# Gate products in four column groups with a summing product, the choice of expert behind the attention scores, memory rows spread one pair of values later

## The chip, the cores and the metric

The kernel runs on one core of a Trainium2 chip. The core has five engines that run their own instruction streams and wait for each other by semaphores: TensorE (PE, matrix products; its weight loads are listed as PEld), VectorE (DVE), ScalarE (ACT), GpSimd (POOL) and SyncE (SP, here only a queue of transfers). The metric is the device time of one execution in microseconds (us); lower is better. A tile below is 128 tokens.

## The reference, cut to what matters

The reference is a chunked attention followed by a mixture of experts with one expert a token.

```python
# attention: q, k, v (4, 8, 768, 64); mem_k, mem_v (4, 8, 8, 64); chunks of 32, context 16 left, 8 right
k_full = np.concatenate([mem_k, k_ctx], axis=2)
a = softmax(scale * q_c @ k_full^T);  out_c = a @ v_full
# moe: x (3072, 512), 8 experts, F = 512
h_dense = np.maximum(x @ w1_dense, 0.0);  y_dense = h_dense @ w2_dense
logits = x @ w_gate                      # (3072, 8), float32
expert_idx = np.argmax(logits, axis=1)
gate_w = 1 / sum(exp(logits - max))
y = y_dense + gate_w * (relu(x @ w1[e]) @ w2[e])     # e = expert_idx of the token
```

## The kernel before, in words

The program has two stages. The first (to about 155 us) computes the attention of 24 tiles of 128 tokens (four batches of six), the gate and the first dense product, and scatters each token's row to a table in memory that is ordered by expert. The second fetches 128 rows at a time by expert, multiplies, adds the second dense product and scatters the results to the output. The change touches the first stage only.

The order of all instructions is written by hand; each engine runs its own in the order of the program. The loop `for i in range(NT)` over the tiles is a software pipeline: pass i does the scores of tile i, but the values and the normalization of tile i-2, the transposition of x of tile i-3 (LAG_X), the gate of tile i-4 (LAG_G) and the dense product of tile i-5 (LAG_D). In pass i, PE runs in this order:

1. in the passes 2 to 17, one or two sets of twelve transposes that prepare keys (`kb`) or queries (`qb`) of the next batch (L353); their results are copied by ACT, two copies into `kbd` for a set of keys (L366), one into `qT` for a set of queries (L358). The second set of a pass comes at its end;
2. the dense product of tile i-5: four products of 512 columns (L469); ACT applies relu (L471);
3. the gate of tile i-4: for four blocks of 128 features, x is the stationary operand (128 x 128, float32) and the 8 columns of `w_gate` move; the four products sum in a PSUM tile `pg` that holds a group of three tiles (L462);
4. when the gate was the last of its group, `choose` follows on DVE (L484 to L494: maximum, difference, priority, maximum, one-hot `oh`), and on ACT three exponentials that also give the weight of each token (L497);
5. the transposes `turn` of the exponentials of tile i-1 (L411), copied by ACT to `aT` (L413);
6. the scores of tile i (L384, L390; L390 works in four column groups of 32). DVE takes the maximum (L399) and subtracts it (L401), ACT takes the exponential (L406);
7. `turn_x`, the transposes of x of tile i-3 (L449), copied by ACT to `x32` (L451); POOL casts that to bf16 (L454);
8. the values of tile i-2: 32 products in tiles of 64 x 32 (L423), normalized by DVE (L433, L435);
9. in every third pass (6, 9, 12, 15, 18, 21) `ranks`: products with `oh` that count each token's place (L504 to L512); DVE turns it into row numbers (`place`, L520, L523).

A window `vw` holds the values of two tiles (a pair; eight chunks) together with eight memory rows for each chunk. Its rows 32 to 56 are the first 24 rows of the next chunk, so they are copied from the window itself (`shift_v`, L308) and, for the last chunk, from the next window (L311, two copies of 24 x 260 in each odd pass). The windows are filled by transfers on SP's queue (`load_v`, L278); SP has also `spread_mem` (L297), which writes the memory rows, repeated for eight chunks, to a table `mrep` in memory, and the windows from the third on fetch their memory rows from it (L292); the first two take them from the SBUF tile `mtpl` (L287). POOL's queue issues the loads of keys and queries (L239), of expert and dense weights (L94), and the scatters (L529); POOL also casts x into the token's row (`keep_x`, L442, L443).

PSUM tiles of the pool `ps` have four buffers, shared by L353, L411, L390, L449 and the ranks; `pg` and the dense and value results have one buffer each.

Of the kernel before, what the change touches and what calls it, by code (L numbers as in the profile page):

```python
# [10 lines left out]
F32 = mybir.dt.float32  # L11
BF16 = mybir.dt.bfloat16
I32 = mybir.dt.int32
AF = mybir.ActivationFunctionType
# [12 lines left out]
PC = 8  # L27
# [17 lines left out]
GRP = 3  # L45
# [14 lines left out]
def kernel(  # L60
# [151 lines left out]
    with ExitStack() as one:  # L212
# [46 lines left out]
        def load_v(n):  # L259
            if n >= B * NP:  # L260
                return
            b, p = divmod(n, NP)
            vw = vws[n]
            if p == 0:
                for par in range(2):
                    r = 64 * par
                    eng = nc.gpsimd if n else nc.vector
                    eng.memset(vw[r:r + 32, 0, :, :D], 0.0)
                    eng.memset(ves[b][r:r + 32, :, :D], 0.0)
            lo = 1 if p == 0 else 0  # L270
            for par in range(2):
                r = 64 * par
                if p == 0:
                    hs = v[b].rearrange("(a c) s d -> c s a d", c=2)[par]
                    nc.sync.dma_start(vw[r + LEFT:r + 32, 0, :, :D], hs[0:LEFT])
                    nc.sync.dma_start(ves[b][r:r + LEFT, :, :D], hs[S - LEFT:S])
                for hp in range(HP):
                    nc.sync.dma_start(  # L278
                        vw[r:r + 32, lo:, hp, :D],
                        bass.AP(tensor=v.tensor,  # L280
                                offset=v[b, 2 * hp + par, CHUNK * (PC * p + lo) - LEFT, 0].offset,
                                ap=[[D, 32], [CHUNK * D, PC - lo], [1, D]]))
# [12 lines left out]
        def spread_mem():  # L295
            for par in range(2):
                nc.sync.dma_start(  # L297
                    mrep[:, par], mtpl[:, par].rearrange("p h d -> p (h d)")
                    .unsqueeze(1).to_broadcast([B * NMEM, PC, HP * (D + 1)]))

        def shift_v(n, par, last, eng=nc.vector.tensor_copy):
            if not 0 <= n < B * NP:
                return
            b, p = divmod(n, NP)
            r = 64 * par
            vw = vws[n]
            if not last:
                eng(vw[r + 32:r + 56, :PC - 1], vw[r:r + 24, 1:])  # L308
            else:
                nxt = ves[b][r:r + 24] if p == NP - 1 else vws[n + 1][r:r + 24, 0]  # L310
                eng(vw[r + 32:r + 56, PC - 1], nxt)  # L311

        def shift(i):

# [61 lines left out]
        def attention(g, qT, kbd):  # L376
# [80 lines left out]
                st["x32"], st["xT"] = x32, xT  # L457

            def gate():
                grp, u = st["grp"], st["u"]  # L460
                for d in range(DT):
                    nc.tensor.matmul(grp["pg"][:, u, :], st["x32"][:, d, :], wgate[:, d, :],  # L462
                                     start=(d == 0), stop=(d == DT - 1))

            def dense():
                late = g == NT - 2
                ph = (ps if late else pf).tile([128, F], F32, tag="ps" if late else "ph", name="ph")
                for d in range(DT):
# [2 lines left out]
                nc.scalar.activation(st["row"][:, XW:2 * XW].bitcast(BF16), ph, AF.Relu)  # L471

            return {"dense": dense, "scores": scores, "exp": expo, "turn": turn, "values": values, "norm": norm,
                    "keep_x": keep_x, "turn_x": turn_x, "gate": gate}

        def choose(grp):
            n = grp["n"]
# [15 lines left out]
            oh = small.tile([128, GRP, E], BF16, tag="oh", name="oh")[:, :n]  # L493
            nc.vector.tensor_tensor(oh, pr, wide(pm), ALU.is_equal)  # L494
            ex = small.tile([128, GRP, E], F32, tag="ex", name="ex")[:, :n]
            for u, row in enumerate(grp["rows"]):
                nc.scalar.activation(ex[:, u], df[:, u], AF.Exp, bias=0.0, scale=1.0,  # L497
                                     accum_out=row[:, ROW - 2:ROW - 1])
            grp["oh"] = oh

        def rank(grp, late):
            oh, n = grp["oh"], grp["n"]
# [49 lines left out]
        nc.vector.memset(kbds[0], 0.0)  # L552
        nc.vector.memset(mkbd, 0.0)
        make_identity(nc, identf)
        nc.sync.dma_start(wgate, moe_w_gate.rearrange("(t p) m -> p t m", p=128))
        load_v(1)
        spread_mem()
        turned, steps = transposes(0)
        for n, step in enumerate(steps):
            step()  # L560
# [21 lines left out]
            if 0 <= g < NT:  # L582
                parts[g][part]()

        def gates(g, now=True):
            grp, u = group_of.get(g, (None, 0))
            if grp is None:
                return
            n = grp["n"]
# [3 lines left out]
            if now:  # L593
                pick(g)

        def pick(g):
            grp, u = group_of.get(g, (None, 0))
            if grp is not None and u == grp["n"] - 1:
                grp["rows"] = [tiles[g - u + k]["row"] for k in range(u + 1)]
                choose(grp)  # L600

        def count_rows(cp):
            for t in range(GRP):
# [14 lines left out]
        for i in range(NT):  # L618
# [9 lines left out]
            tiles[i]["grp"], tiles[i]["u"] = group_of[i]  # L628
            for _ in range(qk_at.get(i, 0)):
                load_qk()  # L630
            if i == 3:
                load_w(E, 0)
            if i == 2:
                nc.gpsimd.memset(front_rows(), 1.0)
            if i in W_AT:
                next_w()
            if i == 1:
                load_v(2)
            if i == 1 or i == 3:
                load_v((i + 5) // 2)  # L640
            if i > 3 and i % 2 == 0:
# [30 lines left out]

        n = NT - 1
        early_fetch()
        gates(n - 3, now=False)
        do("keep_x", n - 2)
        do("turn", n)
        pick(n - 3)
        do("values", n - 1)
        do("turn_x", n - 2)  # L680
        do("norm", n - 1)
# [17 lines left out]
        ranks(n - 1)  # L699
        pick(n)  # L700
        scatter(n - 2)
        do("dense", n - 1)
        ranks(n)
# [250 lines left out]
```

## Time and profile before

| | us |
|---|---|
| median of three runs | 260.94 |
| the three runs | 260.94, 265.48, 260.94 |
| the profiled execution | 261.37 |
| its span from first to last instruction | 259.4 |
| attention stage, tiles 4 to 23 | 35 to 153 |

The granted clock of PE was 0.969 on average. The share of the span in which the engines were busy: PE 83%, DVE 64%, ACT 58%, POOL 57%.

Rows of the time line have the start in us from the beginning of the span, the duration from the first to the last instruction of the row, the engine, the line, the operation, what it writes and reads, its shape and the number of instructions; brackets give the idle time of the engine before the row and what ended it. "issue" there means that the engine waited for nothing that the profile shows. Rows of groups by line have the total busy time, the mean duration of one in ns, and the idle time before them. Instructions of PE overlap, so the cost of a block of products is read from the difference of two starts, not from its duration.

### The profile page before, as it was taken

The page shows a single profiled execution, that of the slowest core. Times are in us where ns is not written, and L with a number is a line of the kernel's source. Part 1 is how long each engine was busy: PE and PEld are TensorE (multiplying, and loading weights), DVE is VectorE, ACT ScalarE, POOL GpSimd, SP SyncE. Part 2 cuts the span into 40 slices and gives each one's busy share as a digit, 9 for nine tenths or more (in the row PEclk, how much of TensorE's full clock was granted, in tenths as well). Part 3 has the DMA queues.
Part 4 walks back from the last instruction along what each step waited for, and adds up shares of the span by engine and source line. Part 5 has one row for each costly group of instructions (what it writes and reads, how often), then busy time and mean ns, then how long its engine had stood idle before and what let it go on. Part 6 is the DMA issues. An engine that isn't in the chain of part 4 may idle for free. (4 is left out here: it accounts for less than half of the span.)

```text
span 259.4 us, 9762 instructions
## 1 busy us (share of the span) xinstructions
PE 215.6 (83%) x3843; PEld 160.2 (62%) x3843; DVE 166.3 (64%) x421; ACT 149.3 (58%) x279; POOL 148.1 (57%) x228
## 2 busy tenths in 40 slices
PE   1556869999798998969888797999999997999930
PEld 0335657778676876848666665766657764666610
DVE  7557855898788798997688534874554443555520
ACT  2545766767788677755667363555546654555520
POOL 8928651888576977865767554554545442334420
PEclk9999997999999999976999999999999999999995
DMA  6999996599989896999998484699999999351120
GB/s 82 189 204 171 161 197 112 111 190 179 183 164 198 136 238 148 135 252 248 280 187 162 141 174 180 173 222 297 276 267 217 286 294 290 124 162 56 48 112 3
DMA packets 56257, 47.03 MB, mean 181 GB/s; under 512 B 30190, under 2 KB 48366, under 8 KB 56048
## 3 DMA queue, kind: packets, MB, share of 16 engines
q0 software_dynamic: 22656, 28.38, 56.2%
q1 hardware_dynamic: 33552, 17.99, 29.4%
q8 instruction: 32, 0.52, 0.9%
q14 instruction: 17, 0.14, 0.2%
HBM read 46.60 MB, written 16.29 MB: 242 GB/s over the span
## 5 line engine op out<-in xcount | busy, mean ns | idle before, releaser
L868 POOL DMA_INDIRECT out_dram<-o,to x28 | 31.1, 1111 | 50.9 <-DVE o L866 41.3
L866 DVE TENSOR_TENSOR o<-py,oe 128x512 f32<-128x512 f32 x28 | 19.4, 691 | 30.2 <-ACT oe L864 28.6
L802 ACT COPY xT<-xt 128x512 bf16<-128x512 bf16 x28 | 16.4, 586 | 36.9 <-DVE gw L857 20.5
L529 POOL DMA_INDIRECT xs<-row,si x24 | 27.8, 1160 | 9.9 <-issue 6.3
L842 PE MATMUL py<-wall,h 128*128 128x512 bf16 (+1 forms) x112 | 28.7, 379 | 1.9 <-DMA wall<-in_moe_w_dram 1.9
L454 POOL CAST xT<-x 128x512 bf16<-128x512 f32 x22 | 13.6, 618 | 28.1 <-ACT x L451 27.9
L839 PE MATMUL py<-wall,xT 128*128 128x512 bf16 x112 | 28.8, 379 | 0.0
L462 PEld LDWEIGHTS pg<-wgate,x 128*128 128x128 f32 x192 | 25.9, 198 | 4.4 <-ACT x L451 1.0
L366 ACT COPY kbd<-tp 64x768 bf16<-64x768 bf16 x28 | 22.1, 791 | 7.9 <-DVE kbd L552 4.2
L469 PE MATMUL ph<-wall,xT 128*128 128x512 bf16 x96 | 26.4, 400 | 0.0
L423 PE MATMUL xp<-vw,aT 64*32 64x65 f32 x1280 | 19.8, 233 | 6.9 <-issue 6.4
L462 PE MATMUL pg<-wgate,x 128*128 128x8 f32 x192 | 24.1, 252 | 0.1
L406 ACT ACTIVATE a<-a 128x512 f32<-128x512 f32 x24 | 15.1, 630 | 15.2 <-DVE a L401 13.8
L423 PEld LDWEIGHTS xp<-vw,aT 64*32 64x32 f32 x1280 | 15.4, 109 | 11.3 <-issue 8.8
L399 DVE TENSOR_REDUCE mx<-sc 128x8 f32<-128x512 f32 x24 | 16.6, 691 | 8.0 <-PE sc L390 6.6
L308 DVE COPY vw<-vw 24x1820 f32<-24x1820 f32 x17 | 21.1, 1242 | 0.5
L442 POOL CAST row<-xn 128x512 bf16<-128x512 f32 x24 | 18.6, 775 | 4.8 <-DVE xn L435 4.6
L864 ACT ACTIVATE oe<-py,gw 128x512 f32<-128x512 f32 x28 | 19.4, 693 | 2.9 <-PE py L842 2.9
L411 PE MATMUL ap<-identf,a 128*128 128x128 f32 x96 | 16.6, 300 | 4.2 <-POOL upper L151 2.5
L801 DVE COPY xT<-xt 128x512 bf16<-128x512 bf16 x28 | 11.8, 421 | 10.6 <-PE xt L799 7.3
L826 ACT ACTIVATE h<-ph 128x512 bf16<-128x512 f32 x28 | 16.7, 597 | 3.0 <-PE ph L823 1.8
L823 PEld LDWEIGHTS <-wall 128*128 128x128 bf16 x256 | 15.6, 98 | 4.4 <-issue 1.0
(163 smaller groups left out, 467.3 us busy)
## 6 DMA issues: line engine op xcount, KB each, us to landing
wall<-in_moe_w_dram POOLq DMA_DIRECT2D x16, 512.0 KB
xg<-xs SPq DMA_DIRECT2D x25, 257.0 KB
kb<-in_k_dram POOLq DMA_DIRECT2D x16, 192.0 KB
qb<-in_q_dram POOLq DMA_DIRECT2D x16, 192.0 KB
vw<-in_v_dram SPq DMA_DIRECT2D x48, 64.0 KB
xs<-wall SPq DMA_DIRECT2D x8, 257.0 KB
vw<-in_v_dram SPq DMA_DIRECT2D x32, 56.0 KB
vw<-mrep SPq DMA_DIRECT2D x16, 65.0 KB
```

The costliest lines, as they stand in the source:

```text
L308: eng(vw[r + 32:r + 56, :PC - 1], vw[r:r + 24, 1:])
L366: nc.scalar.copy(dst, tv[r])
L423: nc.tensor.matmul(xp[32 * cc:32 * cc + 32, par, (D + 1) * hp:(D + 1) * (hp + 1)], st["aT"][r, hp, 32 * cc:32 * cc + 32], vw[r, 4 * (g % 2 ...
L442: nc.gpsimd.tensor_copy(row[:, :XW].bitcast(BF16), st["xn"])
L462: nc.tensor.matmul(grp["pg"][:, u, :], st["x32"][:, d, :], wgate[:, d, :], start=(d == 0), stop=(d == DT - 1))
L469: nc.tensor.matmul(ph, st["xT"][:, d, :], wall[:, E, d, :], start=(d == 0), stop=(d == DT - 1))
L529: i = nc.gpsimd.indirect_dma_start(xs[:, :], bass.IndirectOffsetOnAxis(ap=grp["si"][:, u:u + 1], axis=0), row.bitcast(I32), None, bounds_c ...
L839: nc.tensor.matmul(py, xts[j][:, DT + f, :], wall[:, E, DT + f, :], start=(f == 0), stop=(f == FT - 1))
L842: nc.tensor.matmul(py, hs[j][:, f, :], w[:, f, :], start=(f == 0), stop=(f == FT - 1))
L864: nc.scalar.activation(oe, hs[j, False], AF.Copy, scale=gw)
L866: nc.vector.tensor_tensor(o, hs[j, True], oe, ALU.add)
L868: i = nc.gpsimd.indirect_dma_start(out[:, :], bass.IndirectOffsetOnAxis(ap=to, axis=0), o, None, bounds_check=NT * 128 - 1, oob_is_err=False)
```

## The change

The gate's matrix becomes the stationary operand, padded with zeros to 32 columns for each block of 128 features, and x moves. The four products no longer sum: each writes its own 32 partitions of a 128 x 128 region of the `pg` tile, in its own column group. ACT copies that region to SBUF (`gs`, 128 x 128, float32). A product of `gs` with `parts4`, a matrix of ones and zeros that adds the four groups, then gives the eight logits of each token. This summing product (`gate_sum`) and the choice stand behind the scores, ahead of `turn_x`; the exponentials of the choice (`weigh`) stand behind the tile's exponential on ACT. The copies for the last chunk of a window (L311) go from DVE to ACT. `spread_mem` goes from the prologue to pass 1, behind the loads of the third window, which takes its memory rows from `mtpl`. The load of the first dense weights goes behind the first `keep_x` on POOL. The tail after the loop is arranged accordingly.

```diff
-        wgate = c1.tile([128, DT, E], F32, name="wgate")
+        wgate = c1.tile([128, DT, 32], F32, name="wgate")
+        parts4 = c1.tile([128, E], F32, name="parts4")
...
-                if n < 2:
+                if n < 3:
                     nc.sync.dma_start(
                         vw[r + 56:r + 64].rearrange("p c h d -> p c (h d)"),
                         mtpl[m, par].rearrange("p h d -> p (h d)")
...
-                eng(vw[r + 32:r + 56, PC - 1], nxt)
+                nc.scalar.copy(vw[r + 32:r + 56, PC - 1], nxt)
...
             def gate():
-                grp, u = st["grp"], st["u"]
+                gt = st["grp"]["pt"]
                 for d in range(DT):
-                    nc.tensor.matmul(grp["pg"][:, u, :], st["x32"][:, d, :], wgate[:, d, :],
-                                     start=(d == 0), stop=(d == DT - 1))
+                    nc.tensor.matmul(gt[32 * d:32 * d + 32, :], wgate[:, d, :],
+                                     st["x32"][:, d, :], start=True, stop=True,
+                                     tile_position=(0, 32 * d))
+                gs = work.tile([128, 128], F32, tag="gs", name="gs", bufs=2)
+                nc.scalar.copy(gs, gt)
+                st["gs"] = gs
+
+            def gate_sum():
+                nc.tensor.matmul(st["grp"]["pg"][:, st["u"], :], st["gs"], parts4,
+                                 start=True, stop=True)
...
+        def weigh(grp):
             for u, row in enumerate(grp["rows"]):
-                nc.scalar.activation(ex[:, u], df[:, u], AF.Exp, bias=0.0, scale=1.0,
-                                     accum_out=row[:, ROW - 2:ROW - 1])
+                nc.scalar.activation(grp["ex"][:, u], grp["df"][:, u], AF.Exp, bias=0.0,
+                                     scale=1.0, accum_out=row[:, ROW - 2:ROW - 1])
...
+        nc.vector.memset(wgate[:, :, E:], 0.0)
...
-        nc.sync.dma_start(wgate, moe_w_gate.rearrange("(t p) m -> p t m", p=128))
+        nc.vector.reduce_sum(parts4, identf.rearrange("p (j c) -> p c j", c=32)[:, :E, :],
+                             axis=AX.X)
+        nc.sync.dma_start(wgate[:, :, :E], moe_w_gate.rearrange("(t p) m -> p t m", p=128))
         load_v(1)
-        spread_mem()
...
-                grp["pg"] = pg.tile([128, GRP, E], F32, tag="pg", name="pg")[:, :n]
+                t = pg.tile([128, GRP * E + 128], F32, tag="pg", name="pg")
+                grp["pg"] = t[:, :GRP * E].rearrange("p (t e) -> p t e", e=E)[:, :grp["n"]]
+                grp["pt"] = t[:, GRP * E:]
...
-            if i == 3:
-                load_w(E, 0)
...
             if i == 1:
                 load_v(2)
+                spread_mem()
...
             gates(i - LAG_G)
             do("keep_x", i - LAG_X)
+            if i == 3:
+                load_w(E, 0)
             do("turn", i - 1)
             do("scores", i)
+            pick(i - LAG_G)
             do("turn_x", i - LAG_X)
             do("values", i - 2)
             do("norm", i - 2)
             do("exp", i)
+            weights(i - LAG_G)
...
         do("norm", n)
         gates(n - 2)
         do("turn_x", n - 1)
+        pick(n - 2)
...
         gates(n - 1)
         do("turn_x", n)
+        pick(n - 1)
+        weights(n - 1)
...
-        gates(n, now=False)
+        gates(n)
         ranks(n - 1)
         pick(n)
+        weights(n)
```

More of the change, by code (lines that the diff above doesn't have):

```diff
@@ L473, in attention @@
             return {"dense": dense, "scores": scores, "exp": expo, "turn": turn, "values": values, "norm": norm,
-                    "keep_x": keep_x, "turn_x": turn_x, "gate": gate}
+                    "keep_x": keep_x, "turn_x": turn_x, "gate": gate, "gate_sum": gate_sum}
         def choose(grp):
@@ L583, in do, with gates @@
                 parts[g][part]()
-        def gates(g, now=True):
+        def gates(g):
             grp, u = group_of.get(g, (None, 0))
@@ L588, in gates, with weights @@
                 return
-            n = grp["n"]
             if u == 0:
-                grp["pg"] = pg.tile([128, GRP, E], F32, tag="pg", name="pg")[:, :n]
+                t = pg.tile([128, GRP * E + 128], F32, tag="pg", name="pg")
+                grp["pg"] = t[:, :GRP * E].rearrange("p (t e) -> p t e", e=E)[:, :grp["n"]]
+                grp["pt"] = t[:, GRP * E:]
             parts[g]["gate"]()
-            if now:
-                pick(g)
         def pick(g):
             grp, u = group_of.get(g, (None, 0))
-            if grp is not None and u == grp["n"] - 1:
+            if grp is None:
+                return
+            parts[g]["gate_sum"]()
+            if u == grp["n"] - 1:
                 grp["rows"] = [tiles[g - u + k]["row"] for k in range(u + 1)]
                 choose(grp)
+        def weights(g):
+            grp, u = group_of.get(g, (None, 0))
+            if grp is not None and u == grp["n"] - 1:
+                weigh(grp)
         def count_rows(cp):
@@ L674 @@
         early_fetch()
-        gates(n - 3, now=False)
+        gates(n - 3)
         do("keep_x", n - 2)
@@ L678 @@
         pick(n - 3)
+        weights(n - 3)
         do("values", n - 1)
```

2 lines of the change are left out of this document (1 added, 1 removed).

## The prediction, made before the change was run

> **What bounds the kernel now.** I read four views, in this order: the busy time of the engines by stretches, the waits of TensorE (PE) in the attention stage, and then, instruction by instruction, one pass of the loop on PE and on ScalarE (ACT). The first shows where a change to the gate can act. The columns are busy us and instruction counts of PE, its weight loads, VectorE (DVE), ACT and GpSimd (POOL), then the granted clock and the DMA share.
>
> ```profile
> 35.00:153.00 118.00, 104.72 (x2525) 83.20 (x2523) 89.73 (x208) 80.00 (x165) 80.63 (x130) 0.96 0.92 179
> ```
>
> From 35 to 153 us, while the tiles 4 to 23 run, PE works 104.72 of 118 us, ACT only 80.00. What fills the other 13 us of PE:
>
> ```profile
> PE xp L423 <- issue: 5.4, 4, 2.1
> PE sc L390 <- issue: 2.8, 2, 1.9
> PE tp L353 <- issue: 1.5, 1, 1.5
> PE tp L353 <- ACT aT L413: 1.4, 2, 1.1
> ```
>
> 9.7 us of it are "issue": no data was missing. Only 1.4 us are waits for ACT. So PE's own stream sets the pace, and ACT is close behind. One pass without such a wait is tile 11, from its dense product (L469) to the next one:
>
> ```profile
> 72.29 1.04 PE L469 MATMUL ph<-wall,xT 128*128 128x512 bf16 x4
> 73.17 0.95 PE L462 MATMUL pg<-wgate,x 128*128 128x8 f32 x8
> 73.98 0.63 PE L411 MATMUL ap<-identf,a 128*128 128x128 f32 x4
> 74.45 0.25 PE L384 MATMUL sc<-mkbd,qT 128*128 128x16 bf16 x4
> 74.62 0.38 PE L390 MATMUL sc<-kbd,qT 128*32 128x112 bf16 x16
> 74.94 0.66 PE L449 MATMUL xtp<-identf,xn 128*128 128x128 f32 x4
> 75.52 0.94 PE L423 MATMUL xp<-vw,aT 64*32 64x65 f32 x64
> 76.39 0.53 PE L353 MATMUL tp<-ident,qb 128*64 128x128 bf16 x12
> 76.75 0.50 PE L353 MATMUL tp<-ident,kb 128*64 128x128 bf16 x12
> 77.19 0.39 PE L469 MATMUL ph<-wall,xT 128*128 128x512 bf16 x1
> ```
>
> Starts differ by what a block costs PE: the gate 73.98 - 73.17 = 0.81 us, the whole pass 4.90 us, of which each of the two sets of transposes of L353 takes about 0.4; a pass with one set takes 4.5. ACT in the same pass:
>
> ```profile
> 71.77 0.63 ACT L406 ACTIVATE a<-a 128x512 f32<-128x512 f32 x1 [0.31 <-DVE a L401]
> 72.31 0.78 ACT L358 COPY qT<-tp 128x768 bf16<-128x768 bf16 x1
> 72.98 1.60 ACT L366 COPY kbd<-tp 64x768 bf16<-64x768 bf16 x2
> 74.61 0.60 ACT L471 ACTIVATE row<-ph 128x512 bf16<-128x512 f32 x1
> 75.10 0.58 ACT L413 COPY aT<-ap 128x512 f32<-128x512 f32 x1
> 75.69 0.59 ACT L451 COPY x<-xtp 128x512 f32<-128x512 f32 x1
> ```
>
> ACT is busy without a pause from 71.77 to 76.28, and yet nothing on PE waits for it, because PE needs aT and x only a pass later. The change ends that slack.
>
> **The change part by part.** *Gate on PE.* Removed: eight passes (four float32 products, two passes each) with 128-column weights, 0.81 us a tile. Added: eight passes with 32-column weights and 128 moving columns in four column groups, and later two passes with 128-column weights. Nothing in the trace moves float32 in a real product through four column groups, so I bound it. L390 shows column groups side by side: 16 products, 0.32 us. Four float32 blocks of 128 columns take 0.47 us one after the other (L411, 73.98 to 74.45), 0.12 each. All eight side by side in fours: 2 x 0.12 = 0.24; none: 0.94. Changing between whole array and groups costs about 0.1 us each way (L449 to L423 is 0.58, four blocks 0.47). So the gate takes 0.45 us, at most 1.16; I take 0.45, since L390 is the same array split with other data. The summing product is two of L462's eight passes, 0.20, plus 0.10 for a weight load that can't start before its data: 0.30 (0.20 to 0.40). PE saves 0.81 - 0.45 - 0.30 = 0.06 us a tile (at best 0.16), over the 20 tiles with a gate in the loop **-1.2 us**.
>
> The Trainium skill, "TensorE: Matmul & The Clock Gate", Part 3 (packing small matmuls), says that a weight load overlaps running products only when its row group differs; four column groups share all rows. By that rule the gate would run serially, at 1.16 us. The sixteen products of L390 share their rows as well and took 0.32 us, which speaks against it.
>
> *New wait on PE.* The summing product stands between the scores (L390) and turn_x (L449), and reads a copy that ACT makes behind relu (L471). ACT also gets the last-chunk copies of the memory window, two in each odd tile. Prices from the groups by line:
>
> ```profile
> L413 ACT COPY aT<-ap 128x512 f32<-128x512 f32 x24 | 13.9, 579 | 6.3 <-PE ap L411 5.4 <-ACT row L471 0.7
> ...
> L308 ACT COPY vw<-vw 24x1820 f32<-24x1820 f32 x3 | 5.1, 1704 | 0.1
> L311 DVE COPY vw<-vw 24x260 f32<-24x260 f32 x10 | 5.0, 502 | 0.2
> ```
>
> Between 512 and 1820 elements ACT pays 0.86 ns an element, so 128 cost about 0.25 us and 260 about 0.36; I take 0.25 and, as DVE needs 0.50 for the latter, 0.4 (0.36 to 0.5). In tile 11 ACT is free at 74.58, makes two copies (75.38), relu at its pitch of 0.49 (75.87), the gate copy (76.12). PE is ready for the sum at 74.94 - 0.36 = 74.58 by the cheaper gate. It would wait 1.5 us, and turn_x, values, ranks and the next dense product are queued behind it; x, exp and so again ACT wait for turn_x. So there is now a ring. From one sum to the next: sum 0.30, turn_x until x 0.75, x 0.59, exp 0.54, then the step copies, relu 0.49, gate copy 0.30 with its signal: 2.97 us plus copies (pitches from the rows above: kbd 1.63, qT 0.67, moved pair 0.8). A tile with kbd alone (8, 10, 14, 16): 4.60 against PE's 4.44, +0.15 each; with qT and the pair (7, 9, 13, 15) 4.44, nothing. With qT, kbd and the pair (11, 17): 6.07 against 4.84, +1.2 each. With qT and kbd (6, 12): 5.27 against 4.84, +0.4 each. Together 0.6 + 2.4 + 0.8 = **+3.8 us**. It is 0 if ACT gains on DVE, and 9 if every even tile up to 16 waits some 0.8 and tiles 11 and 17 the whole 1.5. From 18 on there are no step copies.
>
> *Choice behind the scores.* Every third tile five small DVE instructions and the ranks on PE follow. Before (tile 9), on PE and on DVE:
>
> ```profile
> 63.22 0.38 PE L390 MATMUL sc<-kbd,qT 128*32 128x112 bf16 x16
> ...
> 64.99 0.19 PE L504 MATMUL rk<-ecap,ones 128*128 128x24 bf16 x1
> ```
> ```profile
> 63.71 0.18 DVE L484 TENSOR_REDUCE gmx<-pg 128x3 f32<-128x24 f32 x1
> ...
> 64.57 0.18 DVE L494 TENSOR_TENSOR oh<-pr,pm 128x24 bf16<-128x24 f32 x1
> 64.67 0.68 DVE L399 TENSOR_REDUCE mx<-sc 128x8 f32<-128x512 f32 x1
> 65.46 0.69 DVE L401 TENSOR_TENSOR a<-sc,mx 128x512 f32<-128x512 f32 x1
> ```
>
> The choice takes 1.04 us. Now it begins after the subtraction. From the start of the scores: 0.38 for them, 0.09 for the signal (x in tile 11 starts 0.09 after L449's end), 0.79 and 0.70 for maximum and subtraction, 1.04 for the choice: oh at +3.0 us. PE reaches the ranks at +1.77, plus 0.30 for the sum, and some 0.1 of their products needs no oh: it waits 0.85 us, and the second transposes and the next dense product wait behind. Six tiles (6, 9, 12, 15, 18, 21). In 9 and 12 a wait on L353 of 1.5 and 1.1 us (rows above) stands right behind the ranks and is used up by it; 21 has an issue wait before the ranks. Three pay: **+2.5 us** (0 to 5.1). Norm and place on DVE are later by 1.04 too, with over 3 us until the next turn_x, so at no cost. The weights' exponentials leave ACT's place ahead of aT, where they waited for df; that is a gain of ACT's, already in the ring.
>
> *Tail.* The last gate leads over choice, rank and count to the second stage:
>
> ```profile
> 155.41 0.17 PE L512 MATMUL rk<-oh,upper 128*128 128x8 bf16 x1 [0.46 <-DVE oh L494]
> ```
>
> PE waits for that choice already. Gate 0.36 shorter, copy 0.25 and sum 0.30 longer, two signals of 0.1: **+0.4 us** (0 to 0.8). The second stage is unchanged and follows.
>
> *Moved transfers.* On the SP queue the spreading of memory rows goes behind the next value loads; on POOL's the dense weights go behind the first row copy.
>
> ```profile
> 25.37 1.70 SPq L297 DMA_DIRECT2D mrep<-mtpl  x2
> 27.11 8.90 SPq L278 DMA_DIRECT2D vkeep<-in_v_dram  x8
> ```
> ```profile
> 27.18 0.77 POOL L94 DMA_DIRECT2D wall<-in_moe_w_dense_dram  x1
> 28.65 1.54 POOL L442 CAST row<-xn 128x512 bf16<-128x512 f32 x1 [0.69 <-DVE xn L435]
> ```
> ```profile
> 41.40 1.10 DVE L308 COPY vkeep<-vkeep 24x1820 f32<-24x1820 f32 x1 [1.06 <-DMA vkeep<-mrep]
> ```
>
> The value rows of pair 2 start 1.7 us earlier and lose a trip through memory; the one wait they cause is DVE's 1.06 us at 41.40, at a place where PE is busy: 0 (down to -1.1). The next pair's memory rows now wait for the spread on SP, with the loads of pair 4 behind, whose first use is two pairs of tiles later. The weights leave POOL behind a cast of 1.54 and a small copy, some 3 us later; PE's waits name no dense weights, but no row shows their slack: 0 (up to +3). The pad's memset and the summing matrix on DVE lie under the first loads: 0, at most 0.4 (two like L484).
>
> Sum: -1.2 + 3.8 + 2.5 + 0.4 = **+5.5 us**. The profiled execution took 261.37 us (span 259.4 and 1.97 around it), so 266.9; the median of the runs is 0.43 lower, 266.4. I predict 266.5.
>
> **The rivals.** *Faster: ACT keeps ahead.* DVE loses about 11 us of copies, and the scores no longer queue behind the choice (64.67 could be 63.67 in tile 9). If exp then starts about 1 us earlier, relu and the gate copy are through before PE asks; that decides it, from 1.2 us earlier in the tiles 11 and 17. Then only PE's saving counts, 20 x 0.16 = 3.2, and the stretch at half clock can fall away:
>
> ```profile
> 113.80:117.50 3.70, 3.70 (x32) 2.74 (x21) 3.47 (x9) 2.88 (x4) 3.29 (x6) 0.51 1.15 271
> ```
>
> 3.7 us at 0.51 of the clock would take 1.9 at full: -1.8, and up to -1 of the wait at 41.40. 261.4 - 6.0 = 255.4, by the median 255. Against it: relu in tile 11 waited for the kbd copies, not for exp.
>
> *No change.* The waits fall where PE would wait for issue anyway (9.7 us, among which the additions hide): 261. Against it: those waits stand at few places.
>
> *Slower still: a second half clock.* More pauses of PE bring another stretch like 113.8 to 117.5: +1.9 to 268.5, two 270.5.
>
> *The groups don't run side by side*: 20 x (1.16 + 0.30 - 0.81) = 13, and 2.5 for the ranks: 277. Against it: L390. The rule of the Trainium skill cited above would have it so.
>
> **How the numbers follow.** Forecast 0.50 (its own range 262 to 270; a third of it below +2%), faster 0.23, no change 0.10, half clock 0.10, serial groups 0.07. Two per cent, about what a measurement of this kernel can tell from no change, is 5.2 us: 255.7 and 266.2. Slower by more: 0.33 + 0.10 + 0.07 = 0.50; within: 0.17 + 0.10 = 0.27; faster: 0.23. The range from 254.5 to 272 leaves out the serial groups and the lower half of the faster case.
>
> **What would show it.** Right: the gate's block near 0.45 us, a pause of PE ahead of the summing product in tiles 11 and 17 that ends with the gate copy, a pause ahead of the ranks released by oh, PE's busy time in this stage lower and its span longer. Wrong: relu ending well before the scores, no such pauses, a gate block near 1.1 us, or a new wait for the dense weights near 40 us.

## The result, and the profile after

| | before | after |
|---|---|---|
| median of four runs, us | 260.94 | 271.77 |
| the runs, us | 260.70 to 265.48 | 270.20 to 272.02 |
| the profiled execution, us | 261.37 | 272.02 |
| its span, us | 259.4 | 270.1 |
| tile 5 to tile 23 (18 passes, between their first dense products) | 96.4 | 104.4 |
| tile 23 to the last dense product | 19.4 | 21.2 |

A pass of the loop is named here, as in the prediction, by the tile whose scores it does: "tile 5" is pass 5, which begins with a dense product. The changed kernel takes 1.0405 times as long, with an interval of 1.0356 to 1.0455: 10.7 us more in the span, where 5.5 were forecast. 8.0 of them lie in the 18 passes, 1.8 in the tail; the start has 0.4 and the second stage 0.5. (Comparisons leave disturbed runs out, so a ratio need not be the quotient of two medians.)

One row of the view of stretches for each kernel, from the dense product of tile 5 to that of tile 23: the stretch and its length, then busy us and instructions of PE, PE's weight loads, DVE, ACT and POOL, then the granted clock, the DMA share and GB/s. Before:

```profile
40.59:137.01 96.42, 87.28 (x2124) 69.71 (x2123) 78.26 (x172) 68.33 (x139) 68.75 (x111) 0.96 0.94 183
```

After (line numbers of the changed kernel from here on):

```profile
41.01:145.38 104.37, 86.77 (x2159) 57.79 (x2158) 69.95 (x150) 79.55 (x176) 68.30 (x110) 0.94 0.90 167
```

PE worked half a microsecond less and stood still 8.5 us more: 104.37 - 86.77 = 17.60 against 9.14. DVE lost 8 us of work, ACT got 11. PE's waits in the attention stage after name the two new ones first:

```profile
PE pg L473 <- ACT gs L469: 14.0, 17, 2.9
PE rk L522 <- DVE oh L505: 4.1, 5, 1.3
PE xp L425 <- issue: 3.1, 3, 1.8
PE tp L355 <- issue: 2.8, 1, 2.8
```

14.0 us for the gate's copy at the summing product and 4.1 for the choice at the ranks. The issue waits fell from 10.7 (the 9.7 of the prediction and 1.0 at L604, a product that counts rows) to 5.9, so the sum of the waits grew by less than 18. Tile 11 on PE:

```profile
73.29 1.04 PE L480 MATMUL ph<-wall,xT 128*128 128x512 bf16 x4
74.26 0.43 PE L465 MATMUL pg<-x,wgate 128*32 128x128 f32 x8
74.62 0.66 PE L413 MATMUL ap<-identf,a 128*128 128x128 f32 x4
75.11 0.25 PE L386 MATMUL sc<-mkbd,qT 128*128 128x16 bf16 x4
75.29 0.38 PE L392 MATMUL sc<-kbd,qT 128*32 128x112 bf16 x16
78.55 0.39 PE L473 MATMUL pg<-parts,gs 128*128 128x8 f32 x2 [2.88 <-ACT gs L469]
78.79 0.63 PE L451 MATMUL xtp<-identf,xn 128*128 128x128 f32 x4
```

The gate now costs 74.62 - 74.26 = 0.36 us and the sum 78.79 - 78.55 = 0.24, together 0.60 where the old gate took 0.81. But ahead of the sum PE stands for 2.88 us. ACT in the same pass shows why:

```profile
74.56 0.80 ACT L360 COPY qT<-tp 128x768 bf16<-128x768 bf16 x1 [1.58 <-PE ph L480]
75.26 1.60 ACT L368 COPY kbd<-tp 64x768 bf16<-64x768 bf16 x2
76.88 0.84 ACT L313 COPY vw<-vw 24x260 f32<-24x260 f32 x2
77.74 0.60 ACT L482 ACTIVATE row<-ph 128x512 bf16<-128x512 f32 x1
78.24 0.26 ACT L469 COPY gs<-pg 128x128 f32<-128x128 f32 x1
```

The copy itself takes 0.26 us and its data is there from 74.7 on; it comes last, behind qT, kbd, the moved pair and relu. The same picture stands in passes where the prediction expected nothing. ACT in tile 19:

```profile
123.04 1.71 ACT L310 COPY vw<-vw 24x1820 f32<-24x1820 f32 x1
124.75 0.82 ACT L313 COPY vw<-vw 24x260 f32<-24x260 f32 x2
125.59 0.82 ACT L313 COPY vw<-ve 24x260 f32<-24x260 f32 x2
126.43 0.60 ACT L482 ACTIVATE row<-ph 128x512 bf16<-128x512 f32 x1
126.93 0.26 ACT L469 COPY gs<-pg 128x128 f32<-128x128 f32 x1
```

There are no step copies any more in this pass, but the large window copy (L310, ACT's before as well) and four moved copies: 3.4 us ahead of relu. PE waits 2.07 us for it. The tiles 11, 17, 19, 21 and 23, all odd, hold 2.88 + 1.38 + 2.07 + 1.72 + 1.61 = 9.7 of the 14.0 us; tile 4, the first with a gate, has 1.33.

The ranks, in tile 9, on DVE after:

```profile
66.23 0.17 DVE L495 TENSOR_REDUCE gmx<-pg 128x3 f32<-128x24 f32 x1
...
66.66 0.61 DVE L499 SCALAR_TENSOR_TENSOR pr<-df,prio 128x24 f32<-128x24 f32 x1
...
67.52 0.18 DVE L505 TENSOR_TENSOR oh<-pr,pm 128x24 bf16<-128x24 f32 x1
```

and on PE:

```profile
66.70 0.22 PE L519 MATMUL rk<-oh_sum,ones 128*128 128x24 bf16 x3
67.75 0.19 PE L522 MATMUL rk<-oh,ones 128*128 128x16 bf16 x2 [0.83 <-DVE oh L505]
```

The choice runs from 66.23 to 67.70, 1.47 us where it took 1.04 before, and PE waits 0.83 us for its end.

### The profile page after: what moved, and what is told of

Same layout as the page of the kernel before. It is cut to its first block, busy times and chain, and to the rows that moved or that the text cites. A ratio compares the mean times of both kernels' runs of the same rounds, so it can differ in the third digit from the quotient of the medians.

```text
span 270.1 us, 9922 instructions
## 1 busy us (share of the span) xinstructions
PE 215.0 (80%) x3891; PEld 145.9 (54%) x3891; DVE 157.5 (58%) x399; ACT 164.1 (61%) x327; POOL 148.1 (55%) x228
## 5 line engine op out<-in xcount | busy, mean ns | idle before, releaser
L896 DVE TENSOR_TENSOR o<-py,oe 128x512 f32<-128x512 f32 x28 | 19.4, 691 | 30.0 <-ACT oe L894 28.4
L542 POOL DMA_INDIRECT xs<-row,si x24 | 29.4, 1226 | 11.2 <-issue 7.9
L480 PE MATMUL ph<-wall,xT 128*128 128x512 bf16 x96 | 28.0, 419 | 0.0
L401 DVE TENSOR_REDUCE mx<-sc 128x8 f32<-128x512 f32 x24 | 16.6, 692 | 14.0 <-PE sc L392 13.7
L425 PE MATMUL xp<-vw,aT 64*32 64x65 f32 x1280 | 20.4, 240 | 4.0 <-issue 3.1
L453 ACT COPY x<-xtp 128x512 f32<-128x512 f32 x24 | 14.1, 586 | 12.5 <-PE xtp L451 12.1
L894 ACT ACTIVATE oe<-py,gw 128x512 f32<-128x512 f32 x28 | 19.4, 693 | 3.1 <-PE py L872 3.1
L310 DVE COPY vw<-vw 24x1820 f32<-24x1820 f32 x17 | 20.9, 1231 | 0.5
L473 PE MATMUL pg<-parts,gs 128*128 128x8 f32 x48 | 9.3, 266 | 14.1 <-ACT gs L469 14.0
L482 ACT ACTIVATE row<-ph 128x512 bf16<-128x512 f32 x24 | 14.3, 597 | 8.9 <-PE ph L480 8.3
L444 POOL CAST row<-xn 128x512 bf16<-128x512 f32 x24 | 17.8, 742 | 3.4 <-DVE xn L437 3.1
L360 ACT COPY qT<-tp 128x768 bf16<-128x768 bf16 x16 | 12.7, 795 | 10.6 <-PE tp L355 8.9
```

The costliest lines, as they stand in the source:

```text
L425: nc.tensor.matmul(xp[32 * cc:32 * cc + 32, par, (D + 1) * hp:(D + 1) * (hp + 1)], st["aT"][r, hp, 32 * cc:32 * cc + 32], vw[r, 4 * (g % 2 ...
L444: nc.gpsimd.tensor_copy(row[:, :XW].bitcast(BF16), st["xn"])
L480: nc.tensor.matmul(ph, st["xT"][:, d, :], wall[:, E, d, :], start=(d == 0), stop=(d == DT - 1))
L542: i = nc.gpsimd.indirect_dma_start(xs[:, :], bass.IndirectOffsetOnAxis(ap=grp["si"][:, u:u + 1], axis=0), row.bitcast(I32), None, bounds_c ...
L894: nc.scalar.activation(oe, hs[j, False], AF.Copy, scale=gw)
L896: nc.vector.tensor_tensor(o, hs[j, True], oe, ALU.add)
```

## The experiments

The theories. One: PE waits for gs because ACT works in order, with longer work ahead of that copy. Two: the ranks' wait for the choice is paid in full, and is the larger part of the loss. A rival to both: the waits are only a sign that ACT is the bound, and would come back elsewhere. The moved transfers and the old form of the gate are tried apart.

The runs were made in four groups, each on one chip and beside its own runs of the kernel before. Each row has the median and the range; then, from the profile, the 18 passes from tile 5 to tile 23: length, PE's busy time, what is left, and the granted clock.

| kernel | median (range), us | before beside it | 18 passes | busy | idle | clock |
|---|---|---|---|---|---|---|
| before, first profile | 260.94 (260.70-265.48) | | 96.4 | 87.3 | 9.1 | 0.96 |
| changed, first profile | 271.77 (270.20-272.02) | 260.94 | 104.4 | 86.8 | 17.6 | 0.94 |
| gs on DVE | 264.70 (263.85-266.59) | 260.07 | 98.2 | 84.1 | 14.1 | 0.95 |
| pair on DVE | 267.49 (266.53-273.25) | 260.07 | 97.5 | 82.7 | 14.8 | 0.95 |
| old gate | 265.62 (262.88-269.74) | 260.07 | 102.9 | 91.3 | 11.7 | 0.89 |
| transfers only | 262.28 (259.12-270.25) | 260.07 | 92.2 | 83.2 | 9.0 | 0.99 |
| changed again | 271.37 (269.57-273.27) | 259.93 | 102.6 | 87.0 | 15.6 | 0.94 |
| ranks late | 263.27 (262.98-269.78) | 259.93 | 99.5 | 87.4 | 12.1 | 0.91 |
| gs on DVE, ranks late | 261.58 (255.72-266.59) | 259.93 | 96.6 | 84.7 | 11.9 | 0.96 |
| gs on DVE, choice early | 264.54 (262.32-267.33) | 259.93 | 99.1 | 86.2 | 12.9 | 0.97 |
| sum later | 263.05 (259.54-268.30) | 257.93 | 96.8 | 88.9 | 7.9 | 0.93 |
| sum later, pair on DVE | 264.60 (259.98-267.80) | 257.93 | 99.8 | 91.3 | 8.5 | 0.90 |
| the same, transfers back | 262.32 (258.92-264.60) | 257.93 | 97.4 | 88.8 | 8.7 | 0.94 |
| before again | 263.63 (261.97-264.01) | 262.74 | 97.1 | 88.7 | 8.5 | 0.95 |

In the profiles of the four kernels from "gs on DVE" to "transfers only", 17 to 19 of the 72 dense products of these passes have no record, so their busy time is too low and their idle time too high. With the missing ones put in at the records of their weight loads, 0.38 us each, I estimate 12.2, 11.9, 9.9 and 7.1 us of idle time.

On the later chips the kernel before itself ranged from 254.15 to 269.17 us, with mean clocks from 0.92 to 0.98. How little such ratios say below 2% is shown by the last row, so it comes first.

**Before, again.** No edit.

> The kernel before once more with a second profile, as a control. The versions without the two waits need 97 us from tile 5 to tile 23 in their profiles, no more than the 96.4 of the kernel before in its first profile, and yet came out 1.5 to 2% above it by their times. If the first profile stands for the kernel, the second one shows 95 to 97 us again with 8 to 10 us of pauses, and those versions lose elsewhere. If the kernel before has shorter executions than the one profiled first (its times reached down to 254 us on the later chips), the second shows 88 to 94 us, with fewer issue waits and less time at half clock. The ratio of the times is 1.00 either way.

The ratio of the kernel to itself came out at 1.0167 (1.0067 to 1.0266): an interval that leaves out 1 for two equal kernels, where 1.00 was expected (the quotient of the two medians is 1.003). Ratios of up to about 2% in these groups are therefore not told apart from no change. The second profile repeats the first, 97.1 us against 96.4 and 8.5 us of idle time against 9.1, so the budget of the kernel before stands:

```profile
38.97:136.09 97.12, 88.66 (x2125) 70.27 (x2122) 77.70 (x173) 69.09 (x139) 70.91 (x111) 0.95 1.00 183
```

**Changed, again.** No edit.

> The changed kernel once more, so that the other three stand beside it on one chip. 270 to 273, some 4% above the kernel before; if the loss were an accident of the order of the half-clock stretches in one profile, it would come out below 267.

271.37 us: the loss repeats on another chip. PE's waits:

```profile
PE pg L473 <- ACT gs L469: 11.4, 15, 2.1
PE xp L425 <- issue: 6.2, 4, 2.8
PE rk L522 <- DVE oh L505: 2.3, 3, 1.0
PE tp L355 <- issue: 2.0, 1, 2.0
PE rk L522 <- DVE pm L503: 1.0, 1, 1.0
```

The pauses ahead of the sum in the tiles 17, 19 and 21 are 1.38, 2.07 and 1.71 us, as in the first profile within 0.01: they follow from the program. Tile 11 has 1.38 instead of 2.88; the 1.58 us in which ACT stood still ahead of qT there (put down to ph) are missing here. So 1.5 us of that pause did not repeat, for a reason that the rows do not show, and the rest is near what the prediction had worked out (1.2). The pause in tile 23 did not repeat either: 0.60 us instead of 1.61.

**gs on DVE.**

```diff
-                nc.scalar.copy(gs, gt)
+                nc.vector.tensor_copy(gs, gt)
```

> The changed kernel with one edit: VectorE instead of ScalarE copies the gate's 128 x 128 result (gs). Theory 1 (the summing product waits for gs because ScalarE does it in order, behind the step copies, the moved pair copies and relu): the 14.0 us of waits at the summing product fall below 4, and the time falls by 7 to 11 us to 261 to 265. Theory 2 (the ranks' wait for the choice, 4.1 us, and what follows from it is the larger part): the waits move elsewhere and the time stays above 268. Theory 3 (PE only pauses where it must, because ScalarE is the bound and would stop PE at the next dependence anyway): the waits at the summing product go, and as much appears ahead of turn_x, turn or the dense product; 268 to 271.

264.70 us, 7 less than the changed kernel's 271.4 to 271.8. The ratio to the kernel before is 1.0239 (1.0144 to 1.0335).

```profile
PE xp L425 <- issue: 5.9, 4, 2.8
PE rk L522 <- DVE oh L505: 4.8, 6, 1.1
PE pg L473 <- DVE gs L469: 2.9, 7, 1.0
PE ph L480 <- ACT vw L313: 1.3, 1, 1.3
```

The wait at the sum falls from 14.0 (11.4) to 2.9 us and only 1.3 of it shows up again elsewhere behind ACT. Theory one holds: it was the order on ACT, not the products, and not ACT as the bound. Theory two had a time above 268 here, so the ranks' wait is not the larger part; it is still there, 4.8 us. The time fell by 7 us where the wait fell by 8.5 to 11, so the wait was not paid in full.

**Pair on DVE.**

```diff
-                nc.scalar.copy(vw[r + 32:r + 56, PC - 1], nxt)
+                eng(vw[r + 32:r + 56, PC - 1], nxt)
```

> The changed kernel with the last-chunk copies back on VectorE. Theory 1 (ScalarE's order ahead of gs): 0.84 us of ScalarE goes in ten odd tiles, and where the summing product paused longest (tiles 11, 17, 19, 21, 23, all odd) each pause shortens by 0.8 or more: 4 to 6 us off, 266 to 268, and one or two of the stretches at half clock go with them. Rival (the copies' home does not matter, VectorE is loaded by 0.5 us each instead): 270 to 272.

267.49 us, ratio 1.0337 (1.0213 to 1.0462): 4 us off, in the range of theory one.

```profile
PE xp L425 <- issue: 7.1, 5, 2.8
PE pg L473 <- ACT gs L469: 6.5, 11, 1.1
PE rk L522 <- DVE oh L505: 4.5, 5, 1.7
```

Half of the wait for gs goes with copies that take ACT 0.84 us a pass. The longest pause is 1.1, and in each of the tiles 11, 17, 19, 21 and 23 it is 0.86 us or more shorter than in the first profile of the changed kernel.

**Old gate.** The gate's function as before (x stationary, four products that sum in pg), no gs, no summing product.

> The changed kernel with the old form of the gate (x stationary, four products summing in pg, no gs, no summing product); all else stays: choice behind the scores, pair copies on ScalarE, moved transfers. Theory 1: no wait for gs; PE pays 0.81 instead of 0.36 + 0.24 us a tile, the ranks' waits of about 4 us stay: 262 to 265. Theory 2 (choice and ranks are the larger part): 267 or more. If it comes out at or below 261, the choice behind the scores costs nothing by itself and the whole loss belongs to the new form of the gate.

265.62 us, ratio 1.0250 (1.0134 to 1.0367): 0.6 above the range of theory one, 1.4 below that of theory two.

```profile
PE rk L516 <- DVE oh L499: 5.7, 5, 1.7
PE xp L424 <- DMA ve<-in_v_dram: 3.1, 1, 3.1
```

Without any wait at a sum the ranks wait longer, 5.7 us. So the ranks wait for the choice behind the scores whichever form the gate has. That this wait is what keeps the kernel above the one before is argued: the pair's copies and the transfers are still moved here. The profiled execution is the longest of its four (269.74), with 22.5 of the 102.9 us at half clock, and the late transfer of 3.1 us stands in this profile only; I draw no more from it.

**Transfers only.** The kernel before with `spread_mem` behind `load_v(2)`, `n < 3`, and `load_w(E, 0)` behind `keep_x`.

> The kernel before with the moved transfers alone: the memory rows spread behind the third window's loads, that window filled from the tile in SBUF, the dense weights loaded behind the first row copy. My forecast was 0 (down to -1.1, up to +3): 260 to 261.5. Rival (the early part of the changed kernel lost 0.4 us by tile 5 and the first stretch at half clock doubled there because of the transfers): 262 to 264, with a half-clock stretch of 6.8 us before 45 us.

262.28 us, ratio 1.0103 (1.0030 to 1.0176), which the control does not tell from 1. The median lies in the rival's range, but not its sign: by the profile tile 5 begins at 40.30 (40.59 before) and the first stretch at half clock is 3.4 us as before. In the second profile of the kernel before that stretch is 6.8 us, so it doubles without the moved transfers too.

**Ranks late.** The ranks of a group go one pass back, behind `keep_x` and ahead of `turn`.

```diff
+            ranks(i - LAG_G - 1)
             do("turn", i - 1)
...
-            ranks(i - LAG_G)
```

> The changed kernel with the ranks of a group one pass later, behind the gate's products and ahead of the transposes of the exponentials, when oh has long been there. Theory 2 (the ranks' wait of 4.1 us is paid in full): 4 us less, 267 to 268.5. Rival (in tiles where PE did not wait for oh it arrives at the summing product earlier, and ScalarE's order sets its pace): the waits at the summing product grow by what the ranks' waits lose, 270 to 272.

263.27 us beside 271.37 on the same chip: 8 us, where the theory said 4.

```profile
PE pg L473 <- ACT gs L469: 14.9, 16, 3.2
PE xp L425 <- issue: 2.1, 1, 2.1
```

The ranks' wait is gone, 3.3 us in the profile of the changed kernel on this chip. The waits at the sum do grow by 3.5 us, as the rival said, but the issue waits fall from 8.2 to 2.1 and 0.4. The spans of the two profiles differ by 5.9 us: 0.6 up to tile 5, 3.1 in the 18 passes, 1.4 in the tail, 0.8 behind it. So the place of the ranks costs 8 us, more than the wait that was named for it, and the rival's 270 to 272 is out. How it does so stays open: by these rows what fell on balance is issue waits, and none of these views shows why.

**gs on DVE, ranks late.** Both edits.

> Both: gs copied by VectorE and the ranks one pass later. Theories 1 and 2 together take both waits away: 4.8 us of the ranks' waits on top of the 264.7 of the first experiment, 259.5 to 262. Rival (PE's own stream is the bound once gs is in time, and the ranks' wait was time in which others caught up): 263 to 265.

261.58 us (255.72 to 266.59) beside 259.93 (254.15 to 266.36) of the kernel before: the whole loss is gone within the spread. Two edits undo it, neither of which touches the form of the gate. Alone they took 7 and 8 us off, together some 10 of the 11: their gains overlap, so neither wait can be called the larger part.

```profile
PE xp L425 <- issue: 5.7, 3, 2.7
PE pg L473 <- DVE gs L469: 4.3, 9, 1.3
PE tp L355 <- issue: 3.0, 4, 1.7
```

The largest part of PE's waits is issue again, 8.7 us, where the two profiles of the kernel before have 10.7 and 9.9.

**gs on DVE, choice early.** Sum and choice behind `turn`, ahead of the scores.

```diff
+            pick(i - LAG_G)
             do("scores", i)
-            pick(i - LAG_G)
```

> The changed kernel with gs copied by VectorE and with the summing product and the choice ahead of the scores (behind the transposes of the exponentials) instead of behind them. Theory 2: oh is there before the ranks as in the kernel before, no wait at the ranks; the summing product waits up to 0.3 us a tile for gs, as only the transposes (0.47 us) cover its copy: 260 to 263. Rival (the choice delays maximum and subtraction by 1 us, and the exponentials wait for it on ScalarE): 264 or more.

264.54 us, in the rival's range. The sum waits 9.2 us in 13 passes, 0.7 each where I had put 0.3: 0.5 us of transposes do not cover the copy. And ACT's exponential waits for DVE, 8.7 us, against 0.4 with gs on DVE alone:

```profile
ACT a L408 <- DVE a L403: 8.7, 13, 1.4
```

**Sum later**, and two more: gs on DVE, ranks late, and sum and choice behind `norm`; then with the pair on DVE too; then with the transfers back where the kernel before has them.

```diff
             do("scores", i)
-            pick(i - LAG_G)
...
             do("norm", i - 2)
+            pick(i - LAG_G)
             do("exp", i)
```

> The changed kernel with gs copied by VectorE, the summing product and the choice behind the normalization (so that turn_x and the values cover the copy), and the ranks one pass later. Theory (the two waits are the whole loss, and the gate itself saves PE 0.81 - 0.36 - 0.24 = 0.2 us a tile): neither wait is left, below the 261.6 of the version with gs on VectorE and late ranks, 256 to 260. Rival (with those waits gone PE stops for something else: issue, or ScalarE, now with the pair copies): 260 to 263.

> The same with the last-chunk copies back on VectorE. If ScalarE (83.8 of 110 us busy from 35 to 145 with them) still sets the pace in odd tiles, 1 to 3 us less than the run before it; if VectorE's load decides (80 of 110 us, and 0.5 us a copy comes back), the same or 1 us more.

> The same as the second, with the spreading of memory rows and the load of the dense weights where the kernel before has them: what is left of the change is the gate's form with its copy on VectorE, the late sum and choice and late ranks. The moved transfers alone came out at 1.010 (1.003 to 1.018) of the kernel before. If that is real, 1 to 3 us less than the second run; if it was the spread of the clock between runs, no difference. Against the kernel before: 2 to 4 us faster by the gate's 0.2 us a tile, or the same if the pauses that are left are PE's issue waits, which the saved time only makes longer.

263.05, 264.60 and 262.32 us; ratios 1.0149 (1.0070 to 1.0228), 1.0201 (1.0092 to 1.0310) and 1.0189 (1.0122 to 1.0256). None is faster than the kernel before, and none clearly slower by the control's measure. The theory expected 256 to 260 of the first; that missed. The pair on DVE came out 1.6 us longer, near what was expected if DVE's load decides, and the transfers back took 2.3 off, but both lie within the spread of these runs, some 8 us; the 2 to 4 us below the kernel before that the third might have had did not come. The two waits are all but gone, as was meant. First version:

```profile
PE xp L425 <- issue: 4.4, 5, 2.4
...
PE pg L465 <- DVE df L497: 1.9, 3, 1.3
...
PE pg L473 <- DVE gs L469: 0.3, 2, 0.2
```

Idle time in the 18 passes is 7.9 us, below both profiles of the kernel before (9.1 and 8.5). A new wait of 1.9 us came: the next group's gate writes the pg tile that the later choice still reads. The 0.2 us a tile of PE's saving stand against a lower clock: 12.9 us of these passes run at half clock, against 8.4 and 10.2 in the two profiles of the kernel before, and each costs about half of itself, so 1.3 to 2.3 us more. What this profile loses lies behind the first stage: 106.2 us from the last dense product to the end of the span, against 103.0 and 104.0. A stage that ends earlier meets the expert weights earlier. PE's wait for them, before, in the transfers-only kernel (first stage over at 153) and in this one (at 156), a fence each:

```profile
PE py L842 <- DMA wall<-in_moe_w_dram: 1.9, 2, 1.4
```
```profile
PE py L842 <- DMA wall<-in_moe_w_dram: 5.5, 2, 3.5
```
```profile
PE py L872 <- DMA wall<-in_moe_w_dram: 4.2, 2, 2.6
```

Over all profiles it lies between 0.5 and 5.5 us (0.5 and 2.0 for the changed kernel, whose first stage ends at 165 and 167), highest where the first stage ended earliest; but gs on DVE and pair on DVE have 3.0 and 3.5 with an end at 160, so the end is not all that sets it. Besides, between the end of the first stage and 230 us, 10.2 us run at half clock with transfers only and 3.4 each with gs or the pair on DVE, but none in the kernel before. That the second stage gives back a part of what the first one gains is argued from these rows; no run tried it alone. What decides the 1 to 2% between these versions and the kernel before stays open; with the spread of these chips it isn't even sure that there is a difference.

## Why the prediction was right or wrong

Direction and mechanism were right, and part of the places: PE waits for gs behind ACT's work and for oh behind DVE's. The forecast of +5.5 us was half of what came, +10.7; 271.77 us lies just inside the upper end of the range, 272. That it does is in part luck: the terms for the waits, 6.3 us together, met 18.1 us of waits, and the time grew by less because the issue waits fell, which the sum did not have, and PE saved more than it had.

**The gate on PE.** Forecast 0.45 us for the block and 0.30 for the sum, measured 0.36 and 0.24. So the saving is 0.21 us a tile instead of 0.06. Busy time times clock in the 18 passes fell from 87.28 x 0.96 = 83.8 to 86.77 x 0.94 = 81.6, about 2 us by these rounded clocks, where -1.2 was put for 20 tiles. The rival of serial groups, with 1.16 us for this block, is refuted. The Trainium skill ("TensorE: Matmul & The Clock Gate", Part 3, packing small matmuls) has a weight load overlap running products only when its row group differs; the trace does not agree, for in tile 11 the next three weight loads begin between 74.27 and 74.28 us, while the first product, on the same rows, runs from 74.26 to 74.56.

**The new wait on PE: the step that failed, by its size.** +3.8 was put, and 14.0 us of waits came (11.4 in the second profile). "From 18 on there are no step copies" was true and misled: in the odd passes from 19 on ACT has L310 at 1.71 us and two or four moved copies at 0.41, and the ring was not worked out there. The tiles 19, 21 and 23 cost 2.07 + 1.72 + 1.61 = 5.4 us, in the second profile 2.07 + 1.71 + 0.60 = 4.4. The row of L310 on ACT (three of 1704 ns) stood in the prediction, only to price a copy. Tile 17 came as forecast (1.38 against 1.2), tile 11 too in the second profile; in the first, 1.5 us came on top that did not repeat. The ring's small terms were near: 0.16 us in each of the tiles 8, 10, 14 and 16 (0.15 put), 0.53 and 0.52 in 6 and 12 (0.4 put). The rest are 1.33 in tile 4, which had no term, and some 0.2 us in each of 7, 9, 13 and 15. Against that stand 4.8 us less of issue waits in the first profile, 2.5 less in the second, which the sum did not count; so a part of the rival of no change, waits that fall where PE would have waited anyway, came true as well. The prices were right: the groups by line after,

```profile
L469 ACT COPY gs<-pg 128x128 f32<-128x128 f32 x24 | 6.3, 261 | 0.7 <-PE pg L465 0.6
...
L313 ACT COPY vw<-vw 24x260 f32<-24x260 f32 x10 | 4.1, 405 | 0.2
```

have 0.26 and 0.41 us where 0.25 and 0.40 were estimated.

**The choice behind the scores.** +2.5 put, 4.1 us of waits came (3.3 in the second profile), and 8 us went with them when they were taken away. The step that failed: "in 9 and 12 a wait stands right behind the ranks and is used up by it". Tiles 9 and 12 paid 0.83 and 0.50 us, and no such wait stood behind their ranks. In the second profile of the kernel before, the two waits of 1.5 and 1.1 us are 0.35 us and none: a wait in one profile is not a slack that the next has at the same place. Tiles 6, 15 and 18, which were put down for 0.85 each, paid 0.59, 0.83 and 1.34. Besides, the choice took up to 1.47 instead of 1.04 us (below). That tile 21 would be covered was right: none there.

**The tail.** +0.4 put, +1.8 came. Of that, 1.61 is again the ring, in tile 23, where the moved copies of the last window stand ahead of relu. In the second profiles tile 23 has 0.60, and the tail is 20.5 us against 19.9. The +0.4 had only the last gate's own chain.

**The moved transfers.** 0 was put, and by the transfers-only kernel nothing else can be told from 0.

**The half clock.** One or two more stretches were a rival of their own; they came with the forecast. The prediction read the stretch at 113.8 as 3.7 us long, the length of its row; it lasts to 120.67, 6.8 us, so by the same reckoning it costs 3.4 us and not 1.8. Two rows, before and after:

```profile
113.84:120.67 6.83, 6.83 (x107) 5.32 (x103) 5.25 (x12) 4.18 (x6) 3.48 (x6) 0.50 1.09 268
```
```profile
128.41:131.83 3.42, 3.42 (x60) 1.48 (x46) 2.30 (x3) 1.80 (x4) 2.82 (x3) 0.50 0.93 183
```

From tile 4 to the end of the stage it is 10.2 us before and 17.1 after (13.7 and 17.1 in the second profiles). PE is busy in nearly all of that time, and its dense products start 0.43 us apart in it instead of 0.22, so at most half of the difference is lost: 1.7 to 3.4 us of the 10.7. They did not become fewer where the waits did (20.5 us with gs on DVE), so these runs don't show that the change causes them.

**Faster: ACT keeps ahead.** It would have needed relu and gs done before PE asks. Relu came later, not earlier: 77.74 in tile 11 against 74.61 before, in a pass that starts 1.0 us later; in the second profile 2.95 us after the start of its pass, where it was 2.32 before.

## What to carry to other kernels

When a product is to read a copy that a second engine makes, write out that engine's queue ahead of the copy for every kind of pass, the late ones too; 0.26 us of copy became 14 us of waiting because up to 4 us of other work stood ahead of it. A wait in the list is not a price: the copy on DVE took 7 us off where 11 to 14 us of waits were named, the ranks one pass later took 8 off where 3 to 4 were, and the two gains overlap, so each edit has to be tried, alone and together. And a fraction of a microsecond saved on the bounding engine in each pass can be lost again in the clock and in the next stage's transfers, so ask what would show it before building it.

## What the runs showed of the hardware

- A small DVE instruction with two operands in SBUF waits for a POOL cast. The priority product of the choice takes 0.18 us in most passes. In tile 9 (row above) it began at 66.66 and took 0.61 us, during this cast:

```profile
66.62 0.62 POOL L456 CAST xT<-x 128x512 bf16<-128x512 f32 x1 [1.22 <-ACT x L453]
```

  It ended 0.03 us after the cast. The same happened in tile 15 (103.40, 0.60 us, cast from 103.36 to 103.98), and not in the four other groups of the loop, in which it began ahead of a cast, behind one, or with none near (0.18 us each). The Trainium skill, "SBUF — State Buffer", section "SBUF: two separate sides", says that DVE, with two SBUF inputs, and GpSimd share a port pair that one of them holds for a whole instruction; the trace agrees.
- Eight float32 passes with 32-column weights in four column groups took 0.36 us for 128 moving columns each; four full-width transposes of the same size take 0.49 (74.62 to 75.11).
- Up to the end of the first stage the stretches at half clock are 3.4 us long or a multiple of it, in every profile. In the changed kernel's first profile three of them begin 0.4 to 1.2 us after a pause of PE ahead of the sum (1.38 us to 113.8, 2.07 to 127.2, 1.72 to 138.3), yet none follows the longest pause, 2.88 us to 78.55. With the old gate a stretch of 10.2 us begins at 101.1 though PE had no pause of 1 us in the 13 us ahead of it. The Trainium skill, "TensorE: Matmul & The Clock Gate", Part 1, has the clock drop after an idle window of about 3.4 us that runs freely; the length of the stretches agrees, but the pauses ahead of them were shorter than that, and their length alone does not tell which one brings a drop.
